# A 640-column running sum taken as 512 columns and a turned 128-column strip, in a pair of linear-attention blocks

## The chip, the core and the metric

The kernel runs on one core of one Trainium2 chip. The metric is the device time of the whole program in microseconds (us). TensorE is called PE here, VectorE DVE, ScalarE ACT, GpSimd POOL, and SP is the engine that issues most of the transfers.

## What is computed

Two independent blocks, A and B, have the same shapes and their outputs stand side by side. For each block x is 2048 x 640, wqkv is 640 x 1920, wo is 640 x 640, and there are 32 heads of 20 columns:

```python
qkv = (x @ wqkv).reshape(B, S, 3, H, Dh).transpose(2, 0, 3, 1, 4)
q, k, v = qkv[0], qkv[1], qkv[2]
phi = lambda t: where(t > 0, t + 1, exp(t)) + 1e-6
pq, pk = phi(q), phi(k)
kv = einsum("bhsd,bhse->bhde", pk, v)
z = einsum("bhsd->bhd", pk)
o = einsum("bhqd,bhde->bhqe", pq, kv) / (einsum("bhqd,bhd->bhq", pq, z)[..., None] + 1e-6)
out = o.transpose(0, 2, 1, 3).reshape(B, S, D) @ wo
```

The kernel never forms v. It forms G = x^T phi(k), a 640 x 640 sum over the 2048 tokens, and takes kv from G and the v columns of wqkv afterwards. M = kv @ wo follows from that, and the output is (phi(q) / den) @ M.

## The kernel before, in words

Every matrix is split into a high part in a rounded format and a low part, the remainder, so that one product is three matmuls: high x high, low x high, high x low. In the rows of a profile `xnh, xnl` are the two parts of x, `pkh, pkl` those of phi(k), `wkh, wkl` those of the k weights, `xqh, xql` those of x^T for q. A matmul is named by its output and its operands, the moving one first.

The work runs in this order. **K phase, block A and then block B.** Two token tiles of 128 tokens at a time (`kpair`) the PE computes k in seven steps with a scheme of fewer products (outputs `ka`, `ke`, `kb`), ACT and DVE turn it into phi(k), split it, and POOL adds phi(k) into `zacc` by a transfer. In the places between the steps the PE works on G: four token tiles form a group, there are four groups in a block, and for each group and each of the five 128-row chunks of G the function `gstep` (line 517) runs 12 matmuls (four token tiles, three terms) into one bank of the accumulators. One `gstep` takes 320 columns, one half h of the 640, so a group needs ten. DVE then adds the bank into `gacc` (line 537; ACT copies it for a block's first group). phi(k) of a pair of tiles is laid out by column half: one tile holds half h of both token tiles.

Block A's G is used by `kvmm` (line 544, output `pskv`) within the second `kpair` of block B, because the same `gacc` then takes block B's sum. The last group of block B, the closing run below, has no k steps around it: ten `gstep`s follow each other, and with them the K phase ends.

**Q phase.** q is computed by the PE from `xqh, xql` (output `psq`, lines 938 to 940, 512 columns each, c and k running over five chunks), unit by unit of 512 tokens. Block B's `kvmm2` (line 991, output `pskv`) stands in the first unit, the first of them behind nine `psq` matmuls, and reads all of `gacc`. The output products (`outmm`, line 1248) alternate with the units from then on.

The order in the K phase is not written by hand. `note` records jobs with engine, cost and what they read and write, and `Plan.emit` (line 115) lays them out by due times; PE keeps the order of recording, the other engines take what is due first. So a changed job also moves others on DVE, ACT and SP. Each engine then works in its own order, and an instruction that waits holds up what stands behind it on that engine. Transfers of the SP queue use eight completion counters in turn, so the ninth waits until the first has landed.

The names that the prediction uses: `wq` and `wv` are loads of the q and v weights, `xqs` and `xql` loads of x^T for q, `fdh, fdl` stores of forms of block A's M, `xd<-xl` the store of a low part of x^T that is read back as `xql`, `t` and `d` sums of these forms, `xts` and `xns` loads of x. Most of what the change touches follows.

Of the kernel before, what the change touches and what calls it, by code (L numbers as in the profile page):

```python
# [14 lines left out]
H = 32  # L15
# [203 lines left out]
def tile_linear_attn_pair(ctx: ExitStack, tc: tile.TileContext, ins, out: bass.AP):  # L219
# [46 lines left out]
    gacc = {}  # L266
# [16 lines left out]
    MM, MMS = 0.147, 0.105  # L283
# [54 lines left out]
    zd = [dram.tile([P, 20], F32, name=f"zd{b}") for b in range(NB)]  # L338
    md = [dram.tile([D, D], F32, name=f"md{b}") for b in range(NB)]
# [126 lines left out]
    def kpair(p, fill):  # L466

        b = p // NPB
        first = p % NPB == 0
        if first:  # L470
            z_open(b)
        terms = kterms(kleft(p), wf[b])
        T = [Space("kt", D, ANY) for _ in range(2)]
        E = [Space("ek", D, ANY) for _ in range(2)]
        hl = [pk_space() for _ in range(2)]

        def step(n):
            tm, k, start = terms[n]
            rd = [x for a, w in tm for x in (*a, *w)]

            def products():
                o = BK[k].open(("ka", "ke", "kb")[k]) if start else BK[k].tile
                mms(tm, o[:, :HF], start)

            note("PE", MM * 3 * len(tm), products, [BK[k].all], rd)

        def copy(h, t, k):
            o = T[h][t * HF:t * HF + HF]
            note("ACT", HF, lambda: act(o.f, BK[k].tile[:, :HF], AF.Copy), [o], [BK[k].all])  # L489

        def plus(h, t, k):
            o = T[h][t * HF:t * HF + HF]
            note("DVE", HF, lambda: tt(o.f, BK[k].tile[:, :HF], o.f, op=OP.add), [o], [BK[k].all, o])

        def finish(h):
            e, t = E[h].all, T[h].all
# [3 lines left out]
            pk_split(hl[h][0].all, hl[h][1].all, e, D)  # L500
            z_add(first, zac[b][h].all, e)

        after = {0: [(copy, 0, 0, 0)], 2: [(copy, 1, 0, 0)], 3: [(plus, 0, 0, 2)], 4: [(copy, 1, 1, 0), (plus, 1, 1, 1)],
                 5: [(copy, 0, 1, 0), (finish, 0)], 6: [(plus, 1, 0, 1), (finish, 1)]}
        for n in range(7):
            step(n)
            for f, *a in after.get(n, ()):
                f(*a)
            for f, *a in fill.get(n, ()):
                f(*a)  # L510
        for t in range(2):
            pks[2 * p + t] = [tuple(x[t * HF:t * HF + HF] for x in hl[h]) for h in range(2)]


    gn = [1]

    def gstep(i, h, c):
        b, g = divmod(i, NG)
        k = (3, 4, 5)[gn[0] % 3]
        gn[0] += 1  # L520
        tm, rd = [], []
        for j in range(4):
            n = 4 * i + j
            x = tuple(s[c * P:c * P + P] for s in xns[n])
            tm.append((x, pks[n][h]))
            rd += [*x, *pks[n][h]]
        note("PE", MM * 12, lambda: mms(tm, BK[k].open("psg")[:, :HF], True), [BK[k].all], rd)
        go = G[b, c][h * HF:h * HF + HF]

        def keep():  # L530
            if g == 0 and h == 0:
                gacc[b, c] = base.tile([P, D], F32, name="gacc", tag="gacc", bufs=NC)
            o = gacc[b, c][:, h * HF:(h + 1) * HF]
            if g == 0:
                act(o, BK[k].tile[:, :HF], AF.Copy)
            else:
                tt(o, BK[k].tile[:, :HF], o, op=OP.add)  # L537

        note("DVE" if g else "ACT", HF, keep, [go], [BK[k].all])


    kvt = {}

    def kvmm(g, k):
# [6 lines left out]
        def products():  # L551
            o = BK[k].open("pskv")
            wv = w.all.f.rearrange("p (c e) -> p c e", c=NC)
            for c in range(NC):
                gd = gacc[0, c].rearrange("p (d h) -> p d h", h=H)[:, :, h0:h0 + nh]
# [36 lines left out]
    def zsums(b):  # L592

        z, zt32 = Space("zsum", D, ANY), Space("zturn", D, ANY)
        for h in range(2):
            note("DVE", HF, lambda h=h: tt(z.all.f[:, h * HF:h * HF + HF], zac[b][h].all.f[:, :HF],
                                           zac[b][h].all.f[:, HF:], op=OP.add), [z[h * HF:h * HF + HF]],
                 [zac[b][h].all] + ([G[1, NC - 1].all] if b else []), safe=6.0)
# [139 lines left out]
    pair = {}  # L738

    def plain_phi(n):  # L740
        p, t = divmod(n, 2)
        if t == 0:
            pair[p] = [(Space("ek", D, ANY), Space("kt", D, ANY), *pk_space()) for _ in range(2)]
        if n == 0:
            z_open(0)
        for h in range(2):
            e, s, hi, lo = (x[t * HF:t * HF + HF] for x in pair[p][h])
            k = side[n][h]
            note("ACT", HF, lambda e=e, k=k: act(e.f, BK[k].tile[:, :HF], AF.Exp), [e], [BK[k].all])
            note("ACT", HF, lambda s=s, k=k: act(s.f, BK[k].tile[:, :HF], AF.Relu), [s], [BK[k].all])  # L750
        for h in range(2):
            e, s, hi, lo = (x[t * HF:t * HF + HF] for x in pair[p][h])
            note("DVE", HF, lambda e=e, s=s: stt(e.f, e.f, 1.0, s.f, op0=OP.min, op1=OP.add), [e], [e, s])
            pks.setdefault(n, []).append((hi, lo))
            if t == 1:
                e, s, hi, lo = (x.all for x in pair[p][h])
                pk_split(hi, lo, e, D)
                z_add(p == 0, zac[0][h].all, e)
# [34 lines left out]
    for c in range(NC):  # L793
        gstep(0, 0, c)
    def filled(i, h, where=(1, 3, 4, 5, 6)):
        fill = {}
        for c, n in enumerate(where):
            fill.setdefault(n, []).append((gstep, i, h, c))
        return fill

    LAST = (3, 4, 5, 6, 6)
# [7 lines left out]
    for p in range(4, NPB):  # L809
        i, h = divmod(p - 2, 2)  # L810
        gready(i)
        kpair(p, filled(i, h, *((LAST,) if p == NPB - 1 else ())))
    gready(NG - 1)
    for c in range(NC):
        gstep(NG - 1, 0, c)
    wf[1] = forms("wk", ins[1]["wk"], w_split)
    kpair(NPB, filled(NG - 1, 1))
    place = ((1, 5, 0, 6), (2, 0, 1, 6), (2, 2, 2, 6), (3, 0, 3, 6), (3, 2, 4, 6), (4, 0, 5, 6))
    kvs = {1: [(kvmm, g, (6, 7, 3)[g]) for g in range(3)], 4: [(kvmm, g, (4, 5, 6)[g - 3]) for g in range(3, 6)]}
    for p in range(NPB + 1, NP):  # L820
        if p == NPB + 1:
            fl = kvs
        else:
            i, h = divmod(p - NPB - 2, 2)
            gready(NG + i)
            fl = filled(NG + i, h, *((LAST,) if p in (NPB + 2, NP - 1) else ()))
# [21 lines left out]
    for h in range(2):  # L848
        for c in range(NC):
            gstep(LG, h, c)  # L850
# [140 lines left out]
    def kvmm2(b, g):  # L991
# [4 lines left out]
        for c in range(NC):  # L996
            gd = gacc[b, c].rearrange("p (d h) -> p d h", h=H)[:, :, h0:h0 + nh]
# [31 lines left out]
    raw, ft = {}, {}  # L1029
# [38 lines left out]
    def form_load(b, i):  # L1068
# [3 lines left out]
        elif i == 9:  # L1072
            r = [base.tile([P, HF], F32R, name="fh", tag="gacc", bufs=NC),
                 q2[0].tile([P, HF], F32R, name="fl", tag="f9l", bufs=1)]
        elif i != 7:
            r = [base.tile([P, D], F32R, name=f"f{t}", tag="gacc", bufs=NC) for t in "hl"]
        else:
            r = ft[b, 6]
# [367 lines left out]
```

## Time and profile before

| what | value |
|---|---|
| median of 3 runs | 568.3 us (567.91, 568.30, 568.57) |
| profiled execution | span 567.8 us, from the first to the last instruction; the page gives no other time of it |
| PE busy | 562.1 us (99%) |
| DVE, ACT, POOL busy | 428.8, 363.9, 63.1 us |
| matmuls | 3512, of them 960 of 320 columns for G |
| transfers | 117.64 MB, mean 207 GB/s |

In a row of the groups of instructions stand line, engine, operation, tiles out<-in, shapes, count, then the busy time in us and the mean duration of one in ns. Matmuls overlap, so the mean duration of one (309 ns) is not what one costs in a stream: that is read from the distance of starts. In the chain and in the timeline the first number is the start and the second the duration, both in us. A share of the DMA engines is the mean over the core's 16.

### The profile page before, as it was taken

What the parts mean: (1) busy time and instruction counts of PE and PEld (TensorE: products, weight loads), DVE (VectorE), ACT (ScalarE), POOL (GpSimd) and SP (SyncE); (2) the same over time, 40 slices, a digit from 0 to 9 for tenths busy, and PEclk for the clock granted to TensorE, in tenths of its full rate; (3) what the DMA queues carried; (4) which work ended last, traced back from release to release, by engine and by line L of the source; (5) the groups of instructions that cost most, each with busy time, mean ns of one, the idle gap of its engine ahead of it and who ended that gap; (6) DMA issues with size and microseconds to landing.
All of it is one profiled execution on the core that took longest, in us unless ns stands there. A gap on an engine that the chain in (4) does not pass through costs nothing.

```text
span 567.8 us, 9524 instructions
## 1 busy us (share of the span) xinstructions
PE 562.1 (99%) x3512; PEld 534.0 (94%) x3512; DVE 428.8 (76%) x713; ACT 363.9 (64%) x674; POOL 63.1 (11%) x103
## 2 busy tenths in 40 slices
PE   9999999999999999999999999999999999999997
PEld 7999999999999999999988799898989989898997
DVE  7788687598888757988746798967788685767792
ACT  6778566574688756666436678675767666665551
POOL 0210111110001021110010103120012201001010
PEclk9999999999999999999999999999999999999999
DMA  8994764758849767696999985763363997122022
GB/s 308 348 290 121 185 160 106 240 153 239 271 120 268 193 170 197 189 297 200 338 294 315 357 280 173 261 226 117 111 237 128 344 391 259 47 76 92 1 94 92
DMA packets 68321, 117.64 MB, mean 207 GB/s; under 512 B 6804, under 2 KB 30132, under 8 KB 68276
## 3 DMA queue, kind: packets, MB, share of 16 engines
q1 hardware_dynamic: 59060, 89.74, 48.2%
q0 software_dynamic: 8928, 26.92, 17.1%
q8 instruction: 27, 0.44, 0.3%
q10 hardware_dynamic: 288, 0.39, 0.2%
q14 instruction: 18, 0.15, 0.1%
HBM read 71.13 MB, written 35.41 MB: 188 GB/s over the span
## 4 chain that ended last, share of the span: by engine, by line
PE 98%; DMA 1%; DVE 0%; issue 0%
PE psg L316 25%; PE pa L1248 12%; PE ka L316 10%; PE psq L939 8%; PE psq L940 8%; PE psq L938 8%; PE pe L1248 6%; PE ke L316 5%; PE psk L733 4%; PE psb L1248 4%; PE kb L316 3%; DMA xql<-xd 1%; PE pskv L998 1%; PE pskv L556 1%; PE psm L583 1%; PE psi L647 1%
## 5 line engine op out<-in xcount | busy, mean ns | idle before, releaser
L316 PE MATMUL psg<-pkl,xnh 128*128 128x320 f32 x320 | 98.9, 309 | 0.0
L316 PE MATMUL psg<-pkh,xnh 128*128 128x320 f32 x320 | 98.8, 309 | 0.0
L316 PE MATMUL psg<-pkh,xnl 128*128 128x320 f32 x320 | 98.5, 308 | 0.0
L939 PE MATMUL psq<-xql,wh 128*128 128x512 f32 x200 | 78.0, 390 | 1.0 <-DMA xql<-xd 1.0
L938 PE MATMUL psq<-xqh,wh 128*128 128x512 f32 x200 | 78.5, 392 | 0.0
L940 PE MATMUL psq<-xqh,wl 128*128 128x512 f32 x200 | 78.1, 390 | 0.0
L489 ACT ACTIVATE kt<-ka 128x320 f32<-128x320 f32 x52 | 22.7, 437 | 59.1 <-PE ka L316 59.0
L316 PEld LDWEIGHTS psg<-pkl,xnh 128*128 128x128 f32 x320 | 60.1, 188 | 0.0
L316 PEld LDWEIGHTS psg<-pkh,xnl 128*128 128x128 f32 x320 | 60.1, 188 | 0.0
L316 PEld LDWEIGHTS psg<-pkh,xnh 128*128 128x128 f32 x320 | 60.0, 188 | 0.0
L406 POOL DMA_DIRECT2D zacc<-ek x32 | 26.6, 845 | 236.6 <-DVE ek L499 176.8
L1108 DVE SCALAR_TENSOR_TENSOR pq<-eq,rq 128x512 f32<-128x512 f32 x40 | 27.6, 691 | 30.7 <-ACT rq L1107 30.7
L1106 ACT ACTIVATE eq<-psq 128x512 f32<-128x512 f32 x40 | 23.9, 596 | 38.1 <-PE psq L940 36.0
L537 DVE TENSOR_TENSOR gacc<-psg,gacc 128x320 f32<-128x320 f32 x60 | 29.3, 489 | 23.9 <-PE psg L316 22.9
L939 PEld LDWEIGHTS psq<-xql,wh 128*128 128x128 f32 x200 | 37.6, 188 | 8.6 <-DMA xql<-xd 1.4
L1263 ACT ACTIVATE o<-pa 128x320 f32<-128x320 f32 x64 | 27.9, 438 | 27.7 <-PE pa L1248 27.0
L940 PEld LDWEIGHTS psq<-xqh,wl 128*128 128x128 f32 x200 | 37.5, 188 | 7.9
L938 PEld LDWEIGHTS psq<-xqh,wh 128*128 128x128 f32 x200 | 37.6, 188 | 7.2
L401 ACT ACTIVATE pkh<-ek,epst 128x640 fp32r<-128x640 f32 x32 | 26.5, 828 | 6.9 <-DVE ek L499 6.7
L1248 PE MATMUL pa<-fl,dah 128*128 128x320 f32 x96 | 29.7, 309 | 0.0
L1248 PE MATMUL pa<-fh,dal 128*128 128x320 f32 x96 | 29.6, 309 | 0.0
L1248 PE MATMUL pa<-fh,dah 128*128 128x320 f32 x96 | 29.6, 309 | 0.0
(222 smaller groups left out, 1568.0 us busy)
## 6 DMA issues: line engine op xcount, KB each, us to landing
zacc<-ek POOLq DMA_DIRECT2D x32, 320.0 KB, 4.7
xql<-xd SPq DMA_DIRECT2D x40, 256.0 KB, 5.3
xd<-xl SPq DMA_DIRECT2D x29, 320.0 KB, 3.9
out<-o POOLq DMA_DIRECT2D x28, 320.0 KB, 4.2
xns<-in_A_x SPq DMA_DIRECT2D x16, 320.0 KB, 5.6
xts<-in_B_xt_tiles SPq DMA_DIRECT2D x16, 320.0 KB, 3.8
xns<-in_B_x SPq DMA_DIRECT2D x16, 320.0 KB, 5.5
xqs<-in_A_xt SPq DMA_DIRECT2D x20, 256.0 KB, 5.6
```

Of the source, the lines that this page charges most:

```text
L316: nc.tensor.matmul(o, a.r, w.r, start=start and k == i == 0, stop=k == n - 1 and i == 2, skip_group_check=True)
L401: note("ACT", n + 110, lambda: act(hi.r, p.f, AF.Identity, bias=epst), [hi], [p, K0.all], by=8.0)
L406: note("POOL", 1.0, lambda: nc.gpsimd.dma_start(z.f, p.f, **kw), [z], [p], dma=1.0 if first else 1.86)
L537: tt(o, BK[k].tile[:, :HF], o, op=OP.add)
L733: nc.tensor.matmul(o[h][:, :HF], x[a].r, w[c][h * HF:h * HF + HF].r, start=c == 0 and i == 0, stop=c == NC - 1 and i == 2, skip_group_chec ...
L938: nc.tensor.matmul(o, whi, xhi, start=first, stop=False)
L939: nc.tensor.matmul(o, whi, xlo, start=False, stop=False)
L940: nc.tensor.matmul(o, wlo, xhi, start=False, stop=last)
L1106: nc.scalar.activation(e, ps, AF.Exp)
L1108: nc.vector.scalar_tensor_tensor(pq[u][:, c, :], e, 1.0, r, op0=OP.min, op1=OP.add)
L1248: nc.tensor.matmul(ps, x, y, start=start and n == i == 0, stop=n == len(terms) - 1 and i == 2, skip_group_check=True)
L1263: copy = lambda x, y: nc.scalar.activation(x, y, AF.Copy)
```

## The change

The columns of G are taken as a block of 512 and a strip of 128. For the 512 a set of 12 matmuls per chunk writes 512 columns into a bank, with x as the weights as before (`psg`). For the strip the operands change places: phi(k)'s last 128 columns are the weights and x moves, so the output is the strip turned over, 128 rows by 640 columns, in one set of 256 columns (chunks 0 and 1) and one of 384 (chunks 2 to 4), both named `psr`. Seven sets take the place of ten. Each set is recorded as two halves of six matmuls, token tiles (0, 1) and then (3, 2). `gall` is one tile of five chunks in place of five tiles; the strip is kept turned over in its last 128 columns. At the end of each block `gback` turns it back: one 32 x 32 block transpose on DVE, four stores to memory in runs of 32 elements (`rd<-gt`), and one load into the same columns (`gacc<-rd`). Since a set now reads all 512 columns of phi(k) of one token tile, phi(k) is laid out by token tile instead of by column half. Block A's first three `kvmm` move from behind step 1 to behind step 3 of their `kpair`, and the first `mmm` from step 5 to step 6.

```diff
-    def gstep(i, h, c):
+    WD = 4 * P
+    def gset(i, turn, c0, nc_=1, k=None):
 ...
+        n, lo = (nc_ * P, c0 * P) if turn else (WD, 0)
+        tms = []
         for j in range(4):
-            x = tuple(s[c * P:c * P + P] for s in xns[n])
-            tm.append((x, pks[n][h]))
+            x, y = xns[4 * i + j], pks[4 * i + j]
+            if turn:
+                tms.append((tuple(t[WD:D] for t in y), tuple(t[lo:lo + n] for t in x)))
+            else:
+                tms.append((tuple(t[c0 * P:c0 * P + P] for t in x), tuple(t[0:n] for t in y)))
+        def part(first):
+            js = (0, 1) if first else (3, 2)
 ...
+            note("PE", (0.0137 + n / 2400) * 6, products, [BK[k].all], rd)
 ...
+    def gsteps(i, s, alone=False):
+        if s == 0:
+            x, y, u = gset(i, True, 0, 2), gset(i, True, 2, 3), gset(i, False, 0)
+            v = gset(i, False, 1, k=6 if alone else None)
+            if alone:
+                back = [(gback, i // NG)] if i % NG == NG - 1 else []
+                return {0: [x[0], y[0], u[0], v[0], *x[1:], *y[1:], *u[1:], *back, *v[1:]]}
+            out = {1: [x[0], y[0]], 3: [*x[1:], *y[1:]], 4: u, 5: [v[0]], 6: v[1:]}
+        else:
+            x, y, z = (gset(i, False, c) for c in (2, 3, 4))
+            out = {1: [x[0]], 3: x[1:], 4: y, 5: [z[0]], 6: z[1:]}
+        return out
+    def gback(b):
+        t = Space("gt32", D, ANY)
+        turned = [G[b, c][WD:D] for c in range(NC)]
+        note("DVE", D, lambda: nc.vector.transpose(t.all.f, gall[:, :, WD:]), [t.all], turned)
+        rows = rd[b].rearrange("(j r) n -> r j n", r=32)
+        v = Space("rd", 4)
+        for q in range(4):
+            note("SP", 0.07, lambda q=q: nc.sync.dma_start(
+                rows[:, :, 32 * q:32 * q + 32], t.all.f[32 * q:32 * q + 32].rearrange("r (j s) -> r j s", s=32)),
+                [v[q:q + 1]], [t.all], dma=0.6)
+        note("SP", 0.07, lambda: nc.sync.dma_start(gall[:, :, WD:], rd[b].rearrange("(c p) n -> p c n", p=P)),
+             turned, [v.all], dma=1.0, safe=6.0)
 ...
-    kvs = {1: [(kvmm, g, (6, 7, 3)[g]) for g in range(3)], 4: [(kvmm, g, (4, 5, 6)[g - 3]) for g in range(3, 6)]}
+    kvs = {3: [(kvmm, g, (6, 7, 3)[g]) for g in range(3)], 4: [(kvmm, g, (4, 5, 6)[g - 3]) for g in range(3, 6)]}
```

On the PE, in the first free place of a `kpair` of block A: before, one chunk of G for half the columns, all four token tiles.

```order
L316 MATMUL psg_691<-pkh_394,xnh_419 128x320
L316 MATMUL psg_691<-pkl_405,xnh_419 128x320
L316 MATMUL psg_691<-pkh_394,xnl_432 128x320
L316 MATMUL psg_691<-pkh_394,xnh_452 128x320
L316 MATMUL psg_691<-pkl_405,xnh_452 128x320
L316 MATMUL psg_691<-pkh_394,xnl_466 128x320
L316 MATMUL psg_691<-pkh_492,xnh_474 128x320
L316 MATMUL psg_691<-pkl_513,xnh_474 128x320
L316 MATMUL psg_691<-pkh_492,xnl_488 128x320
L316 MATMUL psg_691<-pkh_492,xnh_486 128x320
L316 MATMUL psg_691<-pkl_513,xnh_486 128x320
L316 MATMUL psg_691<-pkh_492,xnl_500 128x320
```

One bank was filled in one go; after, the same kind of place holds the first halves of the two turned sets (token tiles 0 and 1), and x is the moving operand.

```order
L544 MATMUL psr_858<-xnh_693,pkh_533 128x256
L544 MATMUL psr_858<-xnl_762,pkh_533 128x256
L544 MATMUL psr_858<-xnh_693,pkl_560 128x256
L544 MATMUL psr_858<-xnh_731,pkh_592 128x256
L544 MATMUL psr_858<-xnl_777,pkh_592 128x256
L544 MATMUL psr_858<-xnh_731,pkl_610 128x256
L544 MATMUL psr_867<-xnh_693,pkh_533 128x384
L544 MATMUL psr_867<-xnl_762,pkh_533 128x384
L544 MATMUL psr_867<-xnh_693,pkl_560 128x384
L544 MATMUL psr_867<-xnh_731,pkh_592 128x384
L544 MATMUL psr_867<-xnl_777,pkh_592 128x384
L544 MATMUL psr_867<-xnh_731,pkl_610 128x384
```

Over the program 3512 matmuls become 3224: 36 fewer for each of the eight groups. The columns that move through the array are the same number, 38400 per group.

On SP, at the end of block B, between the loads that the Q phase begins with: before (`xql` is what the first `psq` matmuls read, `wv` what `kvmm2` reads).

```order
L890 DMA xql<-xd_84 128x512 x2
L303 DMA xqs<-in_A_xt 128x512 x4
L890 DMA xql<-xd_84 128x512
L634 DMA fdh_114<-fsh 128x320
L634 DMA fdl_115<-fsl 128x320
L890 DMA xql<-xd_84 128x512
L303 DMA wv<-in_B_wv 128x600
L890 DMA xql<-xd_84 128x512
L303 DMA wv<-in_B_wv 128x600 x3
```

After, the four stores of the turned strip stand behind the second `xql`, and its load behind the fifth.

```order
L932 DMA xql<-xd_85 128x512 x2
L583 DMA rd_96<-gt_3336 32x20x32 x4
L303 DMA xqs<-in_A_xt 128x512
L932 DMA xql<-xd_85 128x512 x2
L679 DMA fdh_117<-fsh 128x320
L679 DMA fdl_118<-fsl 128x320
L303 DMA wv<-in_B_wv 128x600
L932 DMA xql<-xd_85 128x512
L586 DMA gacc<-rd_96 128x5x128
L303 DMA wv<-in_B_wv 128x600 x3
```

So three of the five `xql`, one `xqs`, the last `fdh, fdl` and all `wv` now stand behind the four stores, and three `wv` behind the load.

On DVE, in the closing run: before, one add for each of the last `gstep`s (320 columns), with the splits of `wq` between them and the transpose of `zsum` behind all.

```order
L537 TENSOR_TENSOR gacc<-psg,gacc 128x320 x3
L380 TENSOR_TENSOR d_3642<-m 128x320
L875 TENSOR_TENSOR wl<-wq,wh 128x640
L537 TENSOR_TENSOR gacc<-psg,gacc 128x320
L310 TENSOR_TENSOR fsl<-d_3642,fsh 128x320
```

After, the two turned adds come first and the transpose of the strip directly behind them.

```order
L917 TENSOR_TENSOR wl<-wq,wh 128x640
L557 TENSOR_TENSOR gacc<-psr,gacc 128x2x128
L381 TENSOR_TENSOR d_3325<-m 128x320
L557 TENSOR_TENSOR gacc<-psr,gacc 128x3x128
L579 STREAM_TRANSPOSE gt_3336<-gacc 128x640
L557 TENSOR_TENSOR gacc<-psg,gacc 128x512
L310 TENSOR_TENSOR fsl<-d_3325,fsh 128x320
```

The transpose, and with it the first of the four stores, waits for the sets of 256 and 384 columns, which the PE finishes before the five sets of 512.

More of the change, by code (lines that the diff above doesn't have):

```diff
@@ L594, in zsums @@
         z, zt32 = Space("zsum", D, ANY), Space("zturn", D, ANY)
[L595 to L598, printed above, removed]
+        note("DVE", D, lambda: tt(z.all.f, zac[b][0].all.f, zac[b][1].all.f, op=OP.add), [z.all],
+             [x.all for x in zac[b]] + ([G[1, NC - 1].all] if b else []), safe=6.0)
         part, four = Space("zpart", 20), Space("zfour", 20)
@@ L848, in tile_linear_attn_pair @@
     for h in range(2):
-        for c in range(NC):
-            gstep(LG, h, c)
+        whole(LG, h)
     z_end = zsums(1)
@@ L1027, in store_m @@
         eng.dma_start(*written.pop(0))
-    raw, ft = {}, {}
+    raw, ft, fall = {}, {}, []
     def form_sums1(b, k):
```

119 lines of the change are left out of this document (63 added, 56 removed).

## The prediction

> **What bounds the kernel now.** I read the page's head and chain first, then the waits of the PE, then the chain at the end of block B.
>
> ```profile
> span 567.8 us, 9524 instructions
> PE 562.1 (99%) x3512; PEld 534.0 (94%) x3512; DVE 428.8 (76%) x713; ACT 363.9 (64%) x674; POOL 63.1 (11%) x103
> PEclk9999999999999999999999999999999999999999
> PE 98%; DMA 1%; DVE 0%; issue 0%
> ...
> PE psi L647 <- DVE ones L324: 1.0, 1, 1.0
> PE psq L939 <- DMA xql<-xd: 1.0, 1, 1.0
> ```
>
> The PE is the whole chain, at full clock, and stands still for 2.0 us in all: once at the start and once in the Q phase. So what the PE's stream becomes shorter by is the gain, less every new wait of the PE. Everything else is read as a question of whether it makes the PE wait.
>
> The price of a matmul in the stream, first at 320 and then at 512 columns (a group's mean would show overlapping durations, so I take starts):
>
> ```profile
> 266.36 21.11 PE psg L316 x144
> ...
> 350.39 0.39 PE L938 MATMUL psq<-xqh,wh 128*128 128x512 f32 x1
> ...
> 359.94 0.39 PE L938 MATMUL psq<-xqh,wh 128*128 128x512 f32 x1
> ```
>
> 144 of 320 columns take 21.11 us, 146.6 ns each. Between the two quoted starts stand 42 of 512 columns: 9.55 us, 227.4 ns each. 80.8 ns for 192 more columns is 0.421 ns a column, which leaves 12 ns that a matmul costs whatever its width.
>
> **The change, part by part.**
>
> *The matmuls of G.* On that line 256 columns cost 119.7 ns and 384 cost 173.5 ns. A group was 120 x 146.6 = 17.59 us. It becomes 60 x 227.4 + 12 x 119.7 + 12 x 173.5 = 17.16 us. That is 0.43 us less, 3.4 us over eight groups, or 288 matmuls of 12 ns. The same long run of 512-column matmuls gives 226.7 ns over its last 30 steps by its starts, which would make it 3.8 us. I take 3.5 us. No 256-column matmul stands in the trace: its lower bound is the line, its upper bound the 146.6 ns of the next wider one, 96 x 26.9 ns = 2.6 us dearer. What could stretch it is the weight load that each one needs:
>
> ```profile
> 296.60 0.19 PEld L938 LDWEIGHTS psq<-xqh,wh 128*128 128x128 f32 x1
> 296.71 0.19 PEld L939 LDWEIGHTS psq<-xql,wh 128*128 128x128 f32 x1
> ```
>
> Two loads of 128 columns start 0.11 us apart here although each shows 0.19 us. That is below 119.7 ns, so I take the line.
>
> The Trainium skill weighs against the whole term: "TensorE: Matmul & The Clock Gate", section "Back-to-back issue gap", gives the warm gap as columns / 2.4 plus 2.5 ns, so 288 fewer matmuls would save about 0.7 us. The two prices above differ from that rule by 10 ns a matmul, and the measurement decides; a rival below has this direction.
>
> *DVE and ACT.* Ten adds of 320 columns (489 ns) become five of 512, one of 256 and one of 384. Rows of those widths show 692 and 416 ns, so about 4.4 us in place of 4.9 per group. The transposes are two more of 0.85 us. The engine has room in sum, and the PE waited for none of this before: nothing.
>
> ```profile
> L537 DVE TENSOR_TENSOR gacc<-psg,gacc 128x320 f32<-128x320 f32 x60 | 29.3, 489 | 23.9 <-PE psg L316 22.9
> L1188 DVE TENSOR_TENSOR sr<-sr,pq 128x512 f32<-128x512 f32 x7 | 4.8, 692 | 0.2
> L458 DVE TENSOR_TENSOR xsr<-xts 128x256 f32<-128x256 f32 x26 | 10.8, 416 | 0.0
> 288.83 0.85 DVE L602 STREAM_TRANSPOSE zturn<-zsum 128x640 f32<-128x640 f32 x1
> ```
>
> *phi(k) by token tile.* A set needs all columns of a tile, and the tile finished last comes ready behind step 6 of a `kpair`. Its first reader is the second half of the turned sets behind step 3 of the next. Between them stand the last half set (1.4 us), steps 0 to 3 (27 matmuls, 4.0 us) and the first halves (1.8 us): 7.2 us. Before it was 6.6 us, from step 5: step 6, two `gstep`s, steps 0 and 1. More cover than before, so nothing.
>
> *Turning back in block A.* The load into `gacc` stands on SP behind the store of the second `xl` of the next pair but one, so it waits for that DVE row:
>
> ```profile
> 146.09 0.82 DVE L310 TENSOR_TENSOR xl<-xts,xh 128x640 fp32r<-128x640 f32 x1
> 146.94 0.52 SPq L345 DMA_DIRECT2D xd<-xl  x1
> 152.45 3.15 PE pskv L556 x30
> xql<-xd SPq DMA_DIRECT2D x1, 256.0 KB, 4.9
> ```
>
> So it issues near 147.5 of the old time. `kvmm` stood at 152.45 and moves two steps (15 matmuls, 2.2 us) later, less 0.6 us that the sets between have lost: 154.0. That leaves 6.5 us for a load that resembles the 4.9 us one. No wait, with 1.6 us to spare.
>
> *Turning back in block B.* Here it is close. With the closing run's start as zero, the PE does the turned sets by 6.3 us, DVE adds and transposes until about 8, and the Q phase begins at 17.2 us. `kvmm2`, which needs the returned strip, follows at
>
> ```profile
> 287.47 0.23 PE psq L938
> 289.55 1.05 PE pskv L998 x10
> ```
>
> 2.1 us later, at 19.3. The four stores and the load fall into the stretch in which the DMA engines bring everything for the Q phase. From the first `wq` to the landing of the last `xql`, in the kernel before:
>
> ```profile
> DMA packets 3927, 7.73 MB, mean 342 GB/s; under 512 B 437, under 2 KB 824, under 8 KB 3926
> q1 hardware_dynamic: 3638, 7.06, 85.0%
> q0 software_dynamic: 288, 0.66, 18.3%
> ...
> wq<-in_A_wq SPq DMA_DIRECT2D x5, 320.0 KB, 5.4
> xqs<-in_A_xt SPq DMA_DIRECT2D x5, 256.0 KB, 6.2
> xql<-xd SPq DMA_DIRECT2D x5, 256.0 KB, 4.9
> wv<-in_B_wv SPq DMA_DIRECT2D x4, 300.0 KB, 5.2
> zacc<-ek POOLq DMA_DIRECT2D x2, 320.0 KB, 6.8
> ```
>
> That window is 267 to 289.6 us, 22.6 us with the engines at 103%: full. By the order, the changed kernel moves the same before its strip is back, less three `wv` (0.92 MB), plus 1.5 stores of `fdh, fdl` (0.49 MB) that now fall behind the first `wq`, plus the five new transfers. 0.43 MB less at 7.06 MB per 19.2 us is -1.2 us. The load of 640 rows of 512 bytes costs what the one transfer of such rows costs that stands alone, in a window of 3 us:
>
> ```profile
> DMA packets 656, 0.33 MB, mean 109 GB/s; under 512 B 16, under 2 KB 656, under 8 KB 656
> q1 hardware_dynamic: 656, 0.33, 38.1%
> ```
>
> 1.14 us, 28 ns a packet. The stores are four times 640 runs of 128 bytes, which no row shows. By bytes they cost 1.14 us, by packets 4.5 us. Between this packet and the long window's mean one (85 ns for 1941 bytes) the line has 0.039 ns a byte, so 13 ns for 128 bytes, 2.1 us in all. I take that, since both rows lie on it. Together 22.6 - 1.2 + 2.1 + 1.1 = 24.6 us.
>
> The start: in the built program the first `wq` waits for a DVE row about 6.1 us ahead of the closing run (two sets of 512 and the 18 matmuls of steps 5 and 6 lie between, 8.1 us, and three DVE rows take 2.0 of it), the fourth for the third matmul of the last set ahead of it, 2.0 us ahead. Counted from the fourth, with three `wq` (2.7 us) moved by then, the strip is back at -2.0 - 2.7 + 24.6 = 19.9 us: the PE waits 0.6 us. From the first it would be 18.5, no wait. With 28 ns packets it is 22.3, a wait of 3.0 us. I take 0.5 us. Behind the waiting `kvmm2` stand all `psq`; three `wv` behind the load on SP arrive with it, and the next `kvmm2` is 3 us later, so they add nothing. The engines have a gap just after,
>
> ```profile
> 290.00:295.00 5.00, 5.00 (x32) 4.35 (x31) 2.01 (x6) 2.40 (x5) 1.19 (x3) 1.00 0.70 186
> 309.46 6.55 DMA xql<-xd
> ```
>
> 30% of 5 us free, in which the backlog drains. The old wait of 1.0 us comes from an `xql` that starts when the PE frees its buffer and lands 6.55 us later, a distance that the change leaves. I keep it, with up to 1 us either way.
>
> *The sum.* -3.5 + 0.5 = -3.0 us. The span is 567.8 and would be 564.8. The median of the runs lies 0.5 us above the span, so 565.3 us.
>
> The Trainium skill, "DMA: Bandwidth & Descriptors", section "Specifications", speaks against this: under 512 bytes a transfer reads and writes back what it changes. It gives no price. No row shows a long series of such writes, and the rule is the reason for the slower rival below.
>
> **The rivals.**
> 1. The strip comes late, the PE waits 2.4 to 4.7 us, and the gain is gone. The packets of 128 bytes need 25 to 38 ns then. For it: the full engines. Against it: 28 ns is already the price of four times the bytes. About 567.0 us.
> 2. Slower: a short write costs two passes, 56 ns. The stores then need 8.9 us, the strip is back at 26.7, the PE waits 7.4 us: 572.2 us. It decides from 38 ns on, where the wait is 4.6 us. Against it: nothing measured near it is dearer than its bytes.
> 3. The 256-column matmul costs as much as the 320-column one: 2.6 us back, 567.9 us. Against it: the two weight loads.
> 4. The 12 ns a matmul are no cost of the matmul as such, and G's sets go by their columns alone, which stay 38400 a group. Nothing is saved and 0.5 us is waited: 568.8 us. Against it: the two prices of the trace, which no line through zero fits (512 columns would cost 234.6 ns). By the rule of the Trainium skill's clock gate page above it would be 0.7 us less than that.
>
> **How the numbers follow.** One part in 500, 1.1 us, is about what a measurement here can tell from no change. The forecast (no new wait or one up to 2.4 us: 563.9 to 567.1) gets 0.76, rival 1 0.09, rival 2 0.08, rivals 3 and 4 0.05, other small waits 0.02. Faster is the forecast, 0.76. Same takes rivals 1, 3 and 4 and the rest, 0.16. Slower is rival 2, 0.08. The range goes from 564.0 (no wait, and some of the old 1.0 us gone) to 568.0 (the strip late by packets of 28 ns, 567.8, or rival 3).
>
> **What the changed profile would show.** The distance of `psr` starts, 120 and 174 ns, and of `psg`, 227 ns, shows the first term right. A wait of the PE at the first `pskv` of block B for `gacc<-rd`, and its length, tests the DMA sum; the packets of `rd<-gt` show 13, 28 or 56 ns directly. A wait at block A's `pskv` would mean that the load there was held up longer than I think. A wait of the PE on `pkl` or `pkh` would refute the cover of the new layout. I would be most wrong if the short stores are dear.

## The result, and the profile after

The changed kernel takes 573.43 us (median of four executions, 572.55 to 574.13) where the kernel before takes 568.17 us in the same comparison: a ratio of 1.0092, 95% interval 1.0078 to 1.0106. It is slower by 5.3 us; the forecast was 565.3 us, and the range 564.0 to 568.0 does not hold it.

The page of the changed kernel, profiled in an execution of 573.23 us:

```profile
span 571.5 us, 8956 instructions
...
PE 561.5 (98%) x3224; PEld 512.3 (90%) x3224; DVE 427.4 (75%) x689; ACT 361.8 (63%) x668; POOL 62.9 (11%) x103
...
PEclk9999999999999999999989999999999999999999
...
DMA packets 74879, 118.92 MB, mean 208 GB/s; under 512 B 12084, under 2 KB 36692, under 8 KB 74836
...
PE 94%; DMA 2%; DVE 1%; SPq 1%; ACT 0%; issue 0%
```

There are 288 matmuls fewer, as the change says, but PE's share of the chain that ends last is 94% where it was nearly all of it, and one slice of the granted clock shows an 8. PE's waits in the same execution:

```profile
PE pskv L1040 <- DMA gacc<-rd: 3.4, 1, 3.4
PE pskv L603 <- DMA gacc<-rd: 1.0, 1, 1.0
PE psi L692 <- DVE ones L324: 1.0, 1, 1.0
PE psq L981 <- DMA xql<-xd: 0.6, 1, 0.6
```

Only the third is old. The first two are the strip coming back late, in block B (`kvmm2`, line 1040 now) and in block A (`kvmm`, line 603). The timeline of PE around block B's, start and duration in us, with the wait in brackets:

```profile
288.14 0.50 PE L981 MATMUL psq<-xql,wh 128*128 128x512 f32 x1 [0.65 <-DMA xql<-xd]
...
292.31 2.33 PE L1040 MATMUL pskv<-gacc,wv 128*120 128x120 f32 x10 [3.43 <-DMA gacc<-rd]
...
297.10 1.21 PE L1040 MATMUL pskv<-gacc,wv 128*120 128x120 f32 x10
```

The first ten matmuls behind the long wait take 2.33 us, where ten took 1.05 us before. The same stretch by windows (busy us of each engine, then PEclk, the share of the DMA engines and GB/s) says why:

```profile
290.00:292.00 2.00, 0.00 (x0) 0.00 (x0) 0.00 (x0) 0.00 (x0) 0.00 (x0) 1.00 1.08 356
292.00:294.00 2.00, 1.69 (x8) 1.72 (x9) 0.00 (x0) 0.00 (x0) 0.00 (x0) 0.57 1.04 364
294.00:296.00 2.00, 2.00 (x9) 1.68 (x8) 0.57 (x2) 0.30 (x1) 0.91 (x2) 0.58 1.07 294
296.00:298.00 2.00, 2.00 (x15) 1.79 (x14) 0.28 (x1) 1.08 (x2) 1.31 (x3) 1.00 1.04 275
```

After the wait the PE works at half its clock for 3.4 us, then at full clock again. Ten `pskv` lose 1.28 us by it and the first three `psq` behind them, at 0.38 to 0.44 us in place of 0.23, another 0.57: 1.85 us. So the wait costs 5.3 us, not 3.4.

One correction to what the forecast started from. The kernel before was profiled again, in an execution of 568.17 us, and its span is 566.3 us, not 567.8. In all its timed executions whose span is known, 1.8 to 1.9 us lie outside the span, and the spans are 565.8 to 567.1 us; the first profile showed an execution longer than any of these, and its time is not known. So the 0.5 us that the forecast added to the span was the distance to the time of other executions; its sum is not moved by that, since it comes to the median less 3.0 us all the same. PE's waits in the second one:

```profile
PE psi L647 <- DVE ones L324: 1.0, 1, 1.0
```

The old wait of 1.0 us for `xql`, which the forecast carried over, is missing here, and with it most of the 1.5 us by which the first profile is longer. Spans are held against 566.3 us from here on: the changed kernel's is 5.2 us longer.

### The profile page after: what moved, and what is told of

It is laid out like the page before. It is cut to its first block, busy times and chain, and to the rows that moved or that the text cites. A ratio compares the mean times of both kernels' runs of the same rounds, so it can differ in the third digit from the quotient of the medians.

```text
span 571.5 us, 8956 instructions
## 1 busy us (share of the span) xinstructions
PE 561.5 (98%) x3224; PEld 512.3 (90%) x3224; DVE 427.4 (75%) x689; ACT 361.8 (63%) x668; POOL 62.9 (11%) x103
## 4 chain that ended last, share of the span: by engine, by line
PE 94%; DMA 2%; DVE 1%; SPq 1%; ACT 0%; issue 0%
PE psg L544 16%; PE pa L1293 12%; PE ka L316 9%; PE psq L980 8%; PE psq L982 8%; PE psq L981 8%; PE pe L1293 6%; PE psr L544 5%; PE ke L316 5%; PE psk L778 4%; PE psb L1293 4%; PE kb L316 3%; DMA gacc<-rd 2%; PE pskv L1040 1%; PE pskv L603 1%; PE psm L630 1%
## 5 line engine op out<-in xcount | busy, mean ns | idle before, releaser
L544 PE MATMUL psg<-pkh,xnl 128*128 128x512 f32 x160 | 63.0, 394 | 0.0
L544 PE MATMUL psg<-pkl,xnh 128*128 128x512 f32 x160 | 62.8, 393 | 0.0
L544 PE MATMUL psg<-pkh,xnh 128*128 128x512 f32 x160 | 62.3, 389 | 0.0
L407 POOL DMA_DIRECT2D zacc<-ek x32 | 26.6, 830 | 229.8 <-DVE ek L500 168.0
L544 PEld LDWEIGHTS psg<-pkh,xnl 128*128 128x128 f32 x160 | 30.0, 188 | 6.4
L544 PEld LDWEIGHTS psg<-pkl,xnh 128*128 128x128 f32 x160 | 30.0, 188 | 4.9
L544 PEld LDWEIGHTS psg<-pkh,xnh 128*128 128x128 f32 x160 | 30.1, 188 | 4.7
L500 DVE SCALAR_TENSOR_TENSOR ek<-ek,kt 128x640 f32<-128x640 f32 x26 | 21.4, 822 | 15.9 <-ACT kt L499 15.9
L557 DVE TENSOR_TENSOR gacc<-psg,gacc 128x512 f32<-128x512 f32 x30 | 20.4, 689 | 13.3 <-PE psg L544 13.0
L403 DVE SCALAR_TENSOR_TENSOR pkl<-ek,pkh 128x640 fp32r<-128x640 f32 x32 | 26.2, 820 | 1.4 <-ACT pkh L402 1.4
L1293 PE MATMUL pa<-fm,dah 128*128 128x320 f32 x112 | 26.2, 309 | 0.0
```

What stands on the lines that cost most here:

```text
L403: note("DVE", n, lambda: stt(lo.r, p.f, EPS, hi.f, op0=OP.add, op1=OP.subtract), [lo], [p, hi], by=9.0)
L407: note("POOL", 1.0, lambda: nc.gpsimd.dma_start(z.f, p.f, **kw), [z], [p], dma=1.0 if first else 1.86)
L544: nc.tensor.matmul(o[:, :n], a.r, w.r, start=j == 0 and q == 0, stop=j == 2 and q == 2, skip_group_check=True)
L1293: nc.tensor.matmul(ps, x, y, start=start and n == i == 0, stop=n == len(terms) - 1 and i == 2, skip_group_check=True)
```

## The experiments

The first four kernels ask whether the late strip is the whole loss, and whether the half clock belongs to the wait.

**No turn-back at all.** `gback` is not called, so both blocks' K^T V read a strip that is turned over.

```diff
-                back = [(gback, i // NG)] if i % NG == NG - 1 else []
+                back = []
```

> The turn-back (transposition, four stores, load) is left out in both blocks, so K^T V of both blocks reads a strip that is still turned over; all else is the changed kernel. Theory (the loss is the strip's late return): the waits of 3.4 us ahead of the second block's K^T V and of 1.0 us ahead of the first block's go, and the half clock after the longer one with them (about 1.8 us), so the span is near 571.5 - 6.2 = 565.3 us, the saving of the matmuls alone. The 1.2 us more that the changed kernel takes outside its span tell which they belong to: 565.8 us if they come with the transfers of the strip, 567.0 us if not. Rival (the 512-column and 128-column sets or phi(k) by token tile cost what the columns save): 568 us or more, with no long wait in the trace.

Measured: 566.08 us (565.60 to 566.55), ratio 0.9966, interval 0.9954 to 0.9979; span 564.2 us. The waits for the strip and the half clock are gone:

```profile
PE psi L692 <- DVE ones L324: 1.0, 1, 1.0
```

The theory holds, and the whole loss is the turn-back: 573.43 - 566.08 = 7.35 us. The rest of the change, the wide sets, the turned sets and phi(k) by token tile, gains 2.0 us. Some 1.7 to 2.1 us lie outside the span in every kernel here, so none of the loss is there.

**Block B's products later.**

```diff
-        at(("q", 0, (0, 1, 1, 2, 2, 3)[g], (2, 0, 3, 0, 3, 0)[g]), kvmm2, 1, g)
+        at(("q", 0, (1, 1, 2, 2, 2, 3)[g], (3, 4, 0, 2, 4, 1)[g]), kvmm2, 1, g)
```

> Only the places of the second block's six K^T V products in the first Q unit move, the first of them by six weight triples (4.1 us) and the others by one to four, so that the 3.4 us wait would have ended. Theory: the wait at the second block and the half clock behind it go: span 571.5 - 3.4 - 1.8 = 566.3 us, up to 1 us more where a late low half of x^T takes the wait's place; time 568.0 to 569.0 us with 1.7 us outside the span. Rival (the half clock belongs to something else in that stretch): only the 3.4 us go, about 569.8 us, and the clock's row still shows the dip.

Measured: 572.85 us (572.67 to 574.20). Block B's wait for the strip is gone and the half clock too (the granted clock is 0.999 to 1.0 in these executions), but PE waits elsewhere:

```profile
PE pskv L1040 <- DVE kvt L1044: 2.4, 2, 1.6
PE pskv L603 <- DMA gacc<-rd: 1.5, 1, 1.5
PE psq L981 <- DMA xql<-xd: 1.4, 1, 1.4
```

Both theories miss. Later products now wait for DVE's work on an earlier one (`kvt`), and in the chain ahead of them stand a `wv` load of 5.2 us and, issued when that has landed, a `wo` load of 7.3 us. The 3.4 us became 2.4, with 0.8 us more for `xql`, 0.5 more at block A and a new 0.7 for ACT. Moving the consumer passed the lateness on.

**The gap filled.** Fifteen matmuls whose result nothing uses stand ahead of block B's first product.

```diff
+        if g == 0:
+            for i in range(15):
+                nc.tensor.matmul(ps, whl["q", 0, 0][0][:, :P], xt[0, 0][0], start=True, stop=True)
```

> Fifteen matmuls of 512 columns, whose result nothing uses, stand ahead of the first K^T V product of the second block: 15 x 0.23 = 3.45 us of work in the 3.4 us gap. Theory (the idle gap itself lowers the clock): the clock stays at full speed, the ten matmuls after the gap take 1.05 us rather than 2.33, and the span falls by about 1.8 us to 569.7 us, the time to 571.4 us, though not one of the waited-for transfers comes earlier. Rival (the slow ten matmuls come from contention with the transfers or from their operands): they still take 2.3 us and the time stays at 573.2 us.

Measured: 572.50 us (570.58 to 575.50). The filled stretch of block B, timeline and windows:

```profile
292.62 3.60 PE L1040 MATMUL pskv<-xqh,wh 128*128 128x512 f32 x15
296.16 1.31 PE L1043 MATMUL pskv<-gacc,wv 128*120 128x120 f32 x10
```

```profile
154.00:156.00 2.00, 0.00 (x0) 0.00 (x0) 1.82 (x4) 2.00 (x5) 0.08 (x1) 1.00 1.01 376
156.00:158.00 2.00, 1.79 (x13) 1.80 (x14) 0.19 (x1) 0.52 (x1) 0.00 (x0) 0.78 0.76 257
158.00:160.00 2.00, 2.00 (x12) 2.00 (x12) 0.28 (x2) 0.30 (x1) 0.00 (x0) 0.50 0.54 168
...
292.00:294.00 2.00, 1.95 (x8) 1.61 (x9) 0.81 (x1) 0.00 (x0) 0.58 (x1) 1.00 1.04 382
294.00:296.00 2.00, 2.00 (x10) 1.50 (x8) 0.00 (x0) 0.00 (x0) 0.00 (x0) 1.00 1.08 355
```

At block B the clock stays at 1.00 under the same full DMA engines, and the ten products take 1.31 us, not 2.33. So the idle gap lowers the clock and not the transfers. By chance this execution had the same at block A, where the strip was 2.6 us late and nothing filled the gap: the clock falls to 0.50 there, and the execution took 575.5 us. The other three, without it, took 570.6 to 572.7 us, their median 1.1 us below that of the changed kernel; 1.8 us were expected. So the clock is settled by the profile, while the time saved is only roughly known.

**Copies on the core.** In place of the stores and the load, the transposed tile's sixteen 32-column blocks are copied to their partitions, eight on DVE and eight on ACT.

```diff
-            note("SP", 0.07, lambda q=q: nc.sync.dma_start(rows[:, :, 32 * q:32 * q + 32], ...
-        note("SP", 0.07, lambda: nc.sync.dma_start(gall[:, :, WD:], rd[b].rearrange(...)),
+        for i, (r, s) in enumerate([(r, s) for r in range(4) for s in range(4)]):
+            def move(i=i, r=r, s=s):
+                x = gall[32 * s:32 * s + 32, :, WD + 32 * r:WD + 32 * r + 32]
+                u = t.all.f.rearrange("p (c q) -> p c q", q=P)
+                y = u[32 * r:32 * r + 32, :, 32 * s:32 * s + 32]
+                if i % 2:
+                    act(x, y, AF.Copy)
+                else:
+                    nc.vector.tensor_copy(x, y)
```

> The strip is turned back on the core: after the same transposition, sixteen copies of 32 partitions x 5 x 32, eight on DVE and eight on ACT, put the 32x32 blocks in their places; no DRAM tensor, no stores, no load. By the 32x256 copies of 416 ns in the profile a 160-column one takes some 0.32 us, so 2.6 us on each engine and the strip is back near 276.4 + 2.8 = 279.2 us, 9 us before it is needed. Theory: both waits and the half clock go: span 565.3 us, time 565.8 to 567.0 us as without the turn-back. Rival (the 2.6 us more on DVE and ACT hold up the closing runs' evictions): waits of up to 2.6 us of PE on a bank in each closing run, 568 to 570 us.

Measured: 567.13 us (566.96 to 568.24), ratio 0.9987, interval 0.9978 to 0.9996; span 565.2 us. A copy takes 0.25 us on DVE and 0.335 us on ACT. The time is 0.1 us above the theory's range and below the rival's. No wait for the strip, no half clock; one new wait, for work of DVE as the rival has it, but not for a bank and not in a closing run:

```profile
PE psr L544 <- DVE xnl L310: 0.8, 1, 0.8
```

The other seven ask which part of the turn-back is late, and why.

**Block A's turn-back alone.**

```diff
-                back = [(gback, i // NG)] if i % NG == NG - 1 else []
+                back = [(gback, 0)] if i == NG - 1 else []
```

> The turn-back is left out in the second block alone (its K^T V reads a strip still turned over); the first block's stays as in the changed kernel. Theory: the two costs add. Over the run without any turn-back (566.1 us) the first block costs its wait of 1.0 to 2.6 us, seen in three profiles so far, and the half clock behind it (1.7 us) only when it is a long one: 567.1 to 568.7 us, median near 567.6 us, so that the second block accounts for the other 5 to 6 us. Rival (a late strip in one block also delays what the other needs, or the cost is one of both together): 566.1 or above 569 us.

Measured: 566.64 us (566.16 to 569.92, ten executions). The median is below the theory's range, and between it and the rival's 566.1. Eight of the ten lie at 566.2 to 567.2 us, about 0.4 us above the kernel without turn-back, and the profile, taken of one of these, shows

```profile
PE pskv L603 <- DMA gacc<-rd: 0.4, 1, 0.4
```

The other two lie at 569.9 us with a mean granted clock of 0.997. No profile shows them; a longer wait with one stretch of half clock would give both numbers, as it did at block A in the execution with the filled gap. So block A costs 0.4 us or 3.8 us, by the execution, and block B, by the medians, the other 573.43 - 566.64 = 6.8 us.

**One long store.** The transposed strip is stored in 128 packets of 2560 bytes; it comes back in a wrong order.

```diff
-        for q in range(4):
-            note("SP", 0.07, lambda q=q: nc.sync.dma_start(rows[:, :, 32 * q:32 * q + 32], ..., dma=0.6)
+        note("SP", 0.07, lambda: nc.sync.dma_start(rd[b].rearrange("(p c) n -> p (c n)", c=NC), t.all.f),
+             [v.all], [t.all], dma=2.4)
```

> The transposed strip goes to DRAM in one store of 128 packets of 2560 bytes in place of four stores of 640 packets of 128 bytes, in both blocks, so that it comes back in a wrong order; the load is the same. Theory (what the strip lacks is time on the SP queue, where the four stores take 4.3 us to issue, and two landings of about 6 us one after the other): the load is issued 3 to 4 us earlier, near 282.5 us, the wait at the second block falls to 0 to 1 us and the half clock goes: 567.5 to 569.0 us. Rival (the stretch is bound by the bytes on full DMA engines, not by issues or packets): the same bytes move, the load lands at most 1 us earlier, a wait of over 2.4 us stays, 571 us or more.

Measured: 570.89 us (570.71 to 571.15). SP's and PE's timelines at block B:

```profile
276.55 0.32 SPq L581 DMA_DIRECT2D rd<-gt  x1
...
285.05 0.38 SPq L583 DMA_DIRECT2D gacc<-rd  x1
```

```profile
290.63 2.33 PE L1037 MATMUL pskv<-gacc,wv 128*120 128x120 f32 x10 [3.30 <-DMA gacc<-rd]
```

The theory misses, and what the rival said of the load and the wait came true: the store leaves 1.6 us sooner than the first of the four did, the load 1.0 us sooner, and the wait stays at 3.3 us. Of the 2.5 us gained on the changed kernel 1.7 are its waits at block A and for `xql`, which are not there now. The four issues are a part of block B's loss, not all of it: the load stands behind other transfers.

**The load moved forward.** On SP the load stands ahead of two stores, one `wv` and the last `xql`, which stood ahead of it.

```diff
-                [v[q:q + 1]], [t.all], dma=0.6)
+                [v[q:q + 1]], [t.all], dma=0.6, lat=-7.0 if b else 0.0)
-             turned, [v.all], dma=1.0, safe=6.0)
+             turned, [v.all], dma=1.0, safe=6.0, by=6.0 if b else None)
```

> The changed kernel with one move on the SP queue: in the second block the load of the strip stands right behind the four stores and three x^T transfers, ahead of two 160 KB stores, one wv and the last xql, which stood ahead of it. Theory (the load's place on the queue sets the wait: its last store had moved by 283.8 us in the changed kernel and the load was issued only at 286.03): it is issued near 284.4 us, lands near 290.5, the PE waits about 1.7 us rather than 3.4 and the clock stays at full speed: -1.7 and -1.7 us, less up to 1.5 us more of waiting for the last xql, which is later now: 570.0 to 571.5 us. Rival (the stores' landing sets it): the load is issued near 286 us all the same, waits of 3 us or more in front of pskv stay, and the time is 573 us or more.

Measured: 573.52 us (572.67 to 574.45). The load is issued as early as hoped, and the products now wait for a weight that has been pushed behind it:

```profile
284.67 0.38 SPq L586 DMA_DIRECT2D gacc<-rd  x1
...
286.14 0.49 SPq L303 DMA_DIRECT2D wv<-in_B_wv  x1
```

```profile
292.10 2.33 PE L1040 MATMUL pskv<-gacc,wv 128*120 128x120 f32 x10 [2.66 <-DMA wv<-in_B_wv]
```

The load leaves 1.4 us sooner than in the changed kernel, which refutes the rival's 286 us; but it leaves only as its last store lands (issued at 280.35 us, 4.3 us to landing), so here the stores do set it. The time refutes the theory's gain: what is put behind comes late in its place.

**The stores alone.** In block B the four stores stay, the load is left out, so a turned strip is read; everything else keeps its place on SP.

```diff
-        note("SP", 0.07, lambda: nc.sync.dma_start(gall[:, :, WD:], rd[b].rearrange("(c p) n -> p c n", p=P)),
+        note("SP", 0.07, lambda: b or nc.sync.dma_start(gall[:, :, WD:], rd[b].rearrange("(c p) n -> p c n", p=P)),
```

> The changed kernel without the load of the strip in the second block; the four stores stay, at their place on the SP queue, so K^T V of the second block reads a strip still turned over. It is to be held against the run with the first block's turn-back alone (566.6 us), where the first wv was issued at 281.64 us, and the changed kernel, where it was issued at 285.00. Theory (the four stores of 80 KB hold up the whole SP queue by over 3 us, because each waits for one of eight semaphores in turn while the DMA engines run dry): wv and the last xql are issued at 284.5 to 285.0 us as before, PE waits some 0.6 us for xql and 1 to 2 us for wv though it waits for no strip, 568 to 569.5 us. Rival (the load and its landing alone make the loss, the queue is harmless): 566.3 to 567.2 us, without a wait in the second block.

Measured: 570.15 us (569.27 to 572.62), span of the profiled one 567.4 us against 564.6 us without the stores. Block B waits for no strip, and yet:

```profile
PE pskv L1040 <- DMA wv<-in_B_wv: 1.6, 1, 1.6
...
PE psq L981 <- DMA xql<-xd: 0.3, 1, 0.3
```

So the stores by themselves hold up the queue, and the rival is refuted. By the medians they cost 570.15 - 566.64 = 3.5 us, and the load behind them 573.43 - 570.15 = 3.3 us. The theory's waits came near (1.6 and 0.3 us); the median lies 0.65 us above its range, with two of the six executions at 572.4 and 572.6 us, at mean granted clocks of 0.997 and 0.993. SP's rows in this kernel, in the changed one, and in the one with block A's turn-back alone:

```profile
277.20 4.41 SPq L583 DMA_DIRECT2D rd<-gt  x4
...
284.17 0.44 SPq L303 DMA_DIRECT2D wv<-in_B_wv  x1
```

```profile
278.12 4.32 SPq L583 DMA_DIRECT2D rd<-gt  x4
...
285.00 0.44 SPq L303 DMA_DIRECT2D wv<-in_B_wv  x1
...
286.03 0.56 SPq L586 DMA_DIRECT2D gacc<-rd  x1
```

```profile
281.64 0.33 SPq L303 DMA_DIRECT2D wv<-in_B_wv  x1
```

Four stores of 80 KB keep SP for 4.3 us, and the first `wv` leaves 3.4 us later than without them. Half of the 4.3 us is the fourth store alone, in the changed kernel:

```profile
280.18 2.26 SPq L583 DMA_DIRECT2D rd<-gt  x1
```

What the DMA engines did meanwhile, in windows of the changed kernel and then of the one without block B's turn-back (the last two columns):

```profile
280.00:284.00 4.00, 4.00 (x19) 3.30 (x19) 2.31 (x4) 0.00 (x0) 0.00 (x0) 1.00 0.86 213
284.00:286.00 2.00, 2.00 (x11) 1.64 (x10) 0.08 (x1) 0.00 (x0) 0.00 (x0) 1.00 0.69 100
```

```profile
280.00:284.00 4.00, 4.00 (x19) 3.34 (x18) 1.31 (x2) 0.39 (x1) 0.00 (x0) 1.00 1.02 352
284.00:286.00 2.00, 2.00 (x10) 1.63 (x10) 0.62 (x2) 0.24 (x1) 0.00 (x0) 1.00 1.05 390
```

The engines were not full: 4 x 0.14 + 2 x 0.31 = 1.2 us of all sixteen at least went unused. The 2560 packets themselves, at 13 ns each in the median, are another 2.1 us. Together that is 3.3 us, near the delay of `wv`; the two numbers fit, but no run separates them.

The theory's reason, the eight completion counters that SP's transfers use in turn, does not explain the fourth store. The transfer eight places ahead of it is an `fdl` that was issued at 273.36 us and landed 6.5 us later, at 279.9 us, before this issue began at 280.18. The transfers behind it, from `xqs` at 282.54 us to the load at 286.03, leave one right after the other, about 0.5 us apart, so no counter holds them either. The fourth store takes 2.1 to 3.5 us to issue in all twelve places where these four stores are profiled, and the one long store of the version above took 0.32 us. So the small packets go with the long issue; why it is the fourth, and what it waits for, stays open.

Three versions then look for a turn-back that keeps the 2.0 us.

**Block A's copies on ACT.** The version with sixteen copies, and

```diff
-                if i % 2:
+                if i % 2 or b == 0:
                     act(x, y, AF.Copy)
```

> As the version with sixteen copies on the core, but in the first block all sixteen stand on ACT (16 x 0.335 = 5.4 us) and none on DVE. In that version PE waited 0.8 us for a low half of x that DVE made late, at 165 to 173 us. Theory (DVE is what the first block lacks): that wait goes, 566.1 to 566.7 us. Rival (ACT then delays phi(k)'s evictions between 144 and 152 us, where it was busy throughout): PE waits 0.5 to 2 us on a bank or for the returned strip, 567.1 us or more.

Measured: 568.96 us (568.73 to 569.60), ratio 1.0017. The theory misses: the wait for `xnl` that it laid on DVE's copies grew. The time is in the rival's range, but of its waits only 0.3 us for the strip are there:

```profile
PE psr L544 <- DVE xnl L310: 1.2, 1, 1.2
...
PE pskv L607 <- ACT gacc L587: 0.3, 1, 0.3
```

**Block A through memory, block B by copies.** `gback` takes the stores and the load for b = 0, the sixteen copies for b = 1.

```diff
-    kvs = {3: [(kvmm, g, (6, 7, 3)[g]) for g in range(3)], 4: [(kvmm, g, (4, 5, 6)[g - 3]) for g in range(3, 6)]}
+    kvs = {4: [(kvmm, g, (6, 7, 3)[g]) for g in range(3)], 5: [(kvmm, g, (4, 5, 6)[g - 3]) for g in range(3, 6)]}
```

> The first block's strip goes through DRAM as in the changed kernel, with its K^T V products one step later (steps 4 and 5 of the pair, not 3 and 4: some 2.2 us), the second block's is put in place by the sixteen copies, eight on DVE and eight on ACT. Theory: the first block's wait of 0.4 to 2.6 us is covered by 2.2 us more, and neither engine has more work near the first block: 566.1 to 566.7 us, in nearly all executions at full clock, a gain of 0.3% on the kernel before. Rival (the later products hold up the chain behind them, the products with wo in steps that follow): a new wait of PE ahead of psm or of a bank, 567.5 us or more.

Measured: 567.88 us (566.92 to 571.98, twelve executions, two of them above 570.6), ratio 1.0002, interval 0.9986 to 1.0018. The theory misses, and the rival has the time but not the place: the wait is neither covered nor behind the products.

```profile
PE pskv L617 <- DMA gacc<-rd: 1.5, 1, 1.5
```

In the new order of SP the load is issued at 148.08 us instead of 147.33, and it lands only at 156.0, 7.9 us later. A strip through a busy queue used up the room it was given.

**Block A's copies on POOL.** The version with sixteen copies, and

```diff
+                if b == 0:
+                    nc.gpsimd.tensor_copy(x, y)
+                elif i % 2:
                     act(x, y, AF.Copy)
```

> Sixteen copies on the core again, but in the first block all of them stand on POOL, in the second eight on DVE and eight on ACT. No profile here shows such a copy on POOL. Theory (DVE's and ACT's extra 2 to 5 us after the first block made the low halves of x late): that wait of 0.8 us goes, 566.1 to 566.6 us, if a copy takes POOL under 0.6 us (16 x 0.6 = 9.6 us from 143.7 us, just ahead of the K^T V at 154). Rival: a copy on POOL takes 1 us or more, the strip is back after 159 us and PE waits 5 us or more with a half clock behind: 572 us.

Measured: 565.71 us (565.31 to 565.95), ratio 0.9956, interval 0.9943 to 0.9969; span 564.2 us, that of the kernel without any turn-back. The time is below the theory's range, and the only wait of the PE that is left is the one at the start:

```profile
PE psi L701 <- DVE ones L324: 1.0, 1, 1.0
```

The rows of the transposed tile, ns minimum, median and maximum:

```profile
L587 POOL COPY gacc<-gt x16: 308/315/816, 144.2 to 151.1; 32x160 f32<-32x160 f32 x16
L589 ACT ACTIVATE gacc<-gt x8: 334/336/337, 280.8 to 283.2; 32x160 f32<-32x160 f32 x8
L591 DVE COPY gacc<-gt x8: 247/250/253, 280.8 to 282.6; 32x160 f32<-32x160 f32 x8
```

The sixteen copies on POOL run from 144.19 to 151.9 us, 1.7 us ahead of the products. It turns both strips back and beats both kernels: 2.6 us less than before, 7.7 us less than the changed one.

## Why the prediction was wrong, point by point

- *Matmuls of G, -3.5 us.* Right in sign, -1.9 us in size. From start to start, with what comes next, the 960 matmuls of before sum to 140.4 us (146.2 ns each); now 480 of 512 columns take 110.3 us (229.8 ns), 96 of 384 take 16.8 us (175 ns) and 96 of 256 take 11.3 us (118 ns), 138.5 us in all. The step that failed is the price of 512 columns: 227.4 ns came from the `psq` stream, and in G's sets it is 2.4 ns more, 1.15 us; the rest is before's price, 0.5 ns lower over 960. By the formula of the Trainium skill, "TensorE: Matmul & The Clock Gate", section "Back-to-back issue gap", given there for a single matmul and not for a stream with weight loads, it would have been 0.7 us: the measurement lies between the two.
- *DVE, ACT and the layout of phi(k): nothing.* Right. PE waits for neither `pkl` nor `pkh` in any profile here.
- *Block A: no wait, 1.6 us to spare.* The load left at 147.33 us, as worked out (147.5). It then took 6.7 us to land and not 4.9, the landing of a row taken as its like:

```profile
147.33 6.72 DMA gacc<-rd
154.09 3.41 PE pskv L603 x30
```

  The products would also have started at 153.07 us and not at 154.0, so the room was 5.7 us and not 6.5. The step that failed is the landing time, and that a margin was counted from a median: this wait was 0.4, 0.6, 1.0, 1.1, 1.5 and 2.6 us in six profiles with these stores and this load.
- *Block B: a wait of 0.5 us.* It was 3.4 us. The 13 ns a packet were right. The step that failed is the overlap on the DMA engines: "full" engines and one sum of packet times, 24.6 us, as if SP kept the sixteen engines fed and the strip moved when its turn came. Neither was so. The engines idled 1.2 us while SP issued the small stores, the fourth for 2.26 us. And the load, issued behind others at 286.03 us, needed another 6.2 us: the engines were full again (a share of 1.05) and moved 2.29 MB in that time, of which the strip is 0.33 MB. Of the rest 0.85 MB are `wv`, though only one `wv` of 0.31 MB was issued ahead of the load, so transfers behind it took engine time before it had landed.
- *The half clock* was not in the forecast at all: 1.85 us behind one wait. No row of the first trace had a wait over 1.0 us.
- *The rivals.* Rival 1 named the place and the size of the wait (2.4 to 4.7 us), by packets that would be dear; they were not. Rival 2 named the time, 572.2 us, by a double price of short writes; that price is refuted by the 13 ns. Its time was met by luck, through other costs. The forecast called the short stores its weakest point; they were, but in SP's time to issue them and not in the engines' time for a packet.

The sum of what was missed: 1.6 (matmuls) + 2.9 (block B) + 1.85 (half clock) + 1.0 (block A) + 0.65 (`xql`) = 8.0 us, of 573.4 - 565.3 = 8.1 us.

## What to carry to other kernels

Moving a small tile through memory cost its places on the queue and two landings here, not its bytes: before summing packet times, read how long the issues of such transfers hold the queue, what stands behind them, and what else is under way when the tile's own turn comes. A wait of 3.4 us on the bounding engine cost half as much again in clock. Where a tile only has to change partitions, a few copies on an engine with nothing to do are the cheaper way; here POOL did it in 7.7 us that nobody waited for.

## What was not expected of the hardware

- The granted clock fell to half at PE waits of 2.6, 2.66, 3.3 and 3.43 us and at none of 1.65 us or less in these profiles; each time for 3.4 us, or twice that (6.8 us at the 2.66 us). It fell within the wait in three of them and 0.9 us behind it at the 2.6 us. In the 3.4 us ahead of each fall the PE had stood still for 2.4 to 3.4 us, at the 2.66 us with the wait for `xql` just before. The Trainium skill, "TensorE: Matmul & The Clock Gate", section "What's actually happening", has a clock that halves after an idle window of about 3.4 us and is given back after a busy one of the same length, with windows that run by themselves. The length of the dip agrees; gaps a quarter shorter than a window were enough here.
- A copy of 32 partitions x 160 columns to another group of partitions takes 250 ns on DVE, 335 ns on ACT and 315 ns in the median on POOL, where sixteen in a row took 484 ns each (7.74 us).
- Packets of 128, 512 and 2560 bytes took 13, 27 and 102 ns in the median in the changed kernel. The short ones are cheap for the engines; what they held up was SP, which took 2.1 to 3.5 us to issue the fourth store of 640 of them.
